# A planner that counts a delay between dependent instructions of one engine, in a fused attention and expert kernel

## The chip, the cores and the metric

The kernel runs on one core of a Trainium2 chip. A core has five engines that each work through their own queue of instructions in order: TensorE (PE, matmuls; its weight loads are listed apart as PEld), VectorE (DVE), ScalarE (ACT), GpSimd (POOL) and SyncE (SP, which here only starts transfers). They wait for one another through semaphores. The metric is the device time of one execution in microseconds (us).

## The reference

Three stages follow one another. All values are float32.

```python
# attention with decay: B=4, H=8, S=768, D=48
f = 1.0 / (1.0 + np.exp(-f_logit))
for t in range(S):
    state = f[:, :, t, :, None] * state + einsum('bhd,bhe->bhde', k[:, :, t], v[:, :, t])
    y[:, :, t] = einsum('bhd,bhde->bhe', q[:, :, t], state)
# feed-forward: x is 3072 x 384 (tokens x 8 heads of 48), w_in 384 x 2048, w_out 2048 x 384
h = x @ w_in
x = (maximum(h, 0) + alpha * minimum(h, 0)) @ w_out
# experts: 8 of them, each takes 384 tokens, w1 384 x 1024, w2 1024 x 384
logits = x @ w_gate
for idx in argsort(-logits.flatten()):        # best pairs first
    tok, e = idx // 8, idx % 8
    if tok is unassigned and counts[e] < 384: assign tok to e
out[tokens of e] = maximum(x[tokens of e] @ w1[e], 0) @ w2[e]
```

## The kernel before, in words

**How it is built.** The program is first recorded: every call (`nc.vector.tensor_tensor`, `nc.tensor.matmul`, ...) only makes an object `Op` with its dependences, its engine or two possible engines, a price in ns (`cost`) and a priority (`prio`, small is urgent). `Plan.schedule` then goes through all of them as a list scheduler: again and again it takes, over all engines, the instruction that can start first by its own model; of those that can start at the same time the one with the smaller priority. The order that comes out is the order of each engine's queue. No time of the model enters the program, only this order, the buffers, and which of two engines takes an instruction. An instruction is ready when its producers have ended plus `lag`: 110 to 200 ns where the producer is on another engine (`LAGS`), nothing where it is on the same one. All instructions are recorded through one lambda, so that the trace puts them all to line 206 (210 after the change); L1651 are warming matmuls on a tile of ones (`fill`), which the planner puts into gaps that it expects on PE, and L226 the rectifier.

**Precision.** Matmuls run in fp32r; a float32 operand is split into a high part and a low part (`split`: ScalarE copies the high part, then an engine subtracts it), and three products replace one. The subtraction may go to DVE or to POOL (`low`, `Plan.either`): the planner takes the one that it expects to end it first (`better`), where POOL costs 200 + 2.08 ns an element and DVE 66 + 1/0.96.

**Stages, with the times of the profile.** To about 140 us: attention in 24 chunks of 128 tokens (scans and products on DVE, small matmuls on PE), and beside it the preparation of the feed-forward weights in groups 0 to 7 (`prepare_in`, `prepare_out`): the raw weights are narrowed by two bit instructions each on DVE (`narrow`; SCALAR_TENSOR_TENSOR on `early`, `raw`), then split. `win0`, `wo0`, `win1`, `wo1` ... are the tiles `weights0`, `weights1`, `weights2`, `weights3` ...; `raw2` and `raw3` feed group 1. PE does the first blocks of the feed-forward as their weights come. From 140 to 530 us: blocks 0 to 6 of the feed-forward (384 tokens each): 9 matmuls give a piece of the hidden layer (`bank<-weights,rounded`), ScalarE and DVE rectify it (tile `common`), it is split into `rounded`, and 9 matmuls project it (`bank<-rounded,weights`). Beside it the expert weights are split and written to `wd` in DRAM.

From 530 us: the last block, whose logits come before its rows, and the routing. The assignment is found expert by expert in a chain: `bounds` finds the range of the logits (tile `mm`, two small matmuls with `ident`), then four counts follow, each a compare of all 3072 best logits with 64 thresholds on DVE (`cut`, 128x1536) and 12 matmuls that add them up (`bank<-late`), two matmuls with `pairs` and `ones`, and small DVE instructions; `take` writes the number of the expert, at which SP starts the load of its weights; `lists` makes the list of its tokens (DVE compares, 24 matmuls `bank<-late 128x6`, then `idx`). All these tiles lie in the arena `late`. POOL gathers the tokens from `x2d` in DRAM by `idx`; PE transposes them (`bank<-ident,common`). Experts 0 to 7 follow from 618 us; the chain runs two experts ahead of its use and the lists one ahead, in gaps between the expert's matmuls. The chain of expert 0 has nothing ahead of it but the rows of the last block.

**Priorities.** Attention 0 to 60 by block, weight preparation 15.5, expert p's matmuls 105 + 10p, its chain instructions (for p+2) 99 + 10p, its lists (for p+1) 98.5 + 10p, and what makes its hidden layer (`urgent`) 98 + 10p. Chain 0 has 81, the last block 80, its rows 84, and its hidden layer 70.

Of the kernel before, what the change touches and what calls it, by code (L numbers as in the profile page):

```python
# [71 lines left out]
LOADS = 2  # L72


WINDOW, BUSY = 10240 / 3, 3060.0

LAGS = {"tensor": 200.0, "vector": 165.0, "scalar": 150.0, "gpsimd": 110.0, "sync": 120.0}
# [62 lines left out]
class Plan:  # L140
# [181 lines left out]
    def schedule(self):  # L322
        self.layout()
        ops = self.ops
        for op in ops:
            op.left = len(op.deps | op.soft)
            for d in op.deps | op.soft:
                d.next.append(op)
        for op in ops:
            for a in op.arenas():  # L330
                a.left += 1
        free = dict.fromkeys(self.ENGINES, 600.0)
        free["tensor"] = 800.0
        avail = {e: [] for e in self.ENGINES}
        mm, hw, dma = [0.0, 0.0], 600.0, [0.0, 0.0]

        def offer(op):
            since = max([g.since for g in op.uses if g.slot] + [d.start for d in op.soft], default=0.0)
            op.ready = {e: max([d.end + lag(d, e) + (op.load if d in op.held else 0.0) for d in op.deps], default=since) for e in op.engines}
            for e in op.engines:  # L340
                avail[e].append(op)

        def first(op, e):
            t, taken = max(op.ready[e], free[e]), []
            for a in op.arenas():
                if any(o.left for o in a.over):
                    return None
                t = max([t] + [o.turn for o in a.over])
            for g in op.first:
                p = self.place(g, taken)  # L350
                if p is None:
                    return None
                t = max(t, p[0])
                taken.append(p[1])
            return t

        for op in ops:
            if not op.left:
                offer(op)
        for _ in ops:  # L360
            best = None
            for e in self.ENGINES:
                for op in avail[e]:
                    if best is not None and max(op.ready[e], free[e]) > best[0]:
                        continue
                    t = first(op, e)
                    if t is None or len(op.engines) > 1 and not self.better(op, e, t, free):
                        continue
                    key = (t, op.prio, op.idx)
                    if best is None or key < best[:3]:  # L370
                        best = key + (e, op)
            assert best, "no instruction can start"
            t, _, _, e, op = best
            for x in op.engines:
                avail[x].remove(op)
            for g in op.first:
                g.since, g.slot = self.place(g, ())
                g.slot.busy = True
                g.tag.given += 1
            price = op.cost[e]  # L380
            if e == "tensor":
                self.fill(free[e], t)
                slow = self.slow(t)
                if op.load:
                    mm[1] = max(mm) + op.load * slow
                    t = max(t, mm[1])
                price *= slow
                mm[0] = t
                self.count(t, t + price, op.columns)
            op.engine, op.start = e, t  # L390
            for a in op.arenas():
                a.left, a.turn = a.left - 1, max(a.turn, t + 1.0)
            free[e] = op.end = t + price
            if op.bytes:
                at = op.end
                if e == "sync":
                    hw = at = max(hw, at) + 450.0
                lane = e == "sync"
                dma[lane] = max(dma[lane], at + 650.0) + op.bytes / (300.0 if lane else 200.0)
                op.end = dma[lane] + 1000.0 + op.extra  # L400
            for g in op.uses:
                g.uses -= 1
                g.end = max(g.end, op.end)
                if not g.uses:
                    g.slot.busy, g.slot.free = False, g.end + 100.0
            for n in op.next:
                n.left -= 1
                if not n.left:
                    offer(n)
        return max(op.end for op in ops)  # L410
# [94 lines left out]
def lag(d, e):  # L505

    if d.bytes:
        return 0.0
    if d.engine == e:
        return 0.0  # L510
    return LAGS[d.engine] + (40.0 if e == "gpsimd" else 0.0)


# [1312 lines left out]
```

## Time and profile before

| | us |
|---|---|
| median of 3 runs | 872.51 (870.24 to 876.36) |
| the profiled execution, its own time | 872.57 |
| its span in the profile | 870.6 |
| PE busy | 829.7 |
| DVE busy | 580.2 |
| ScalarE busy | 350.9 |
| GpSimd busy | 118.6 |
| mean granted clock of PE | 0.979 of full |

Busy times add the instructions of an engine; matmuls overlap their neighbours, so a start-to-start distance says more than a duration where they stand in a row. In the rows of a timeline, the first number is the start in us from the beginning of the span, the second the duration (of the whole group where several instructions are put together as xN), then the engine, the line, the operation, output<-inputs by the names of their arenas, and in brackets how long the engine was idle before it and what ended that.

### The profile page before, as it was taken

The numbers are of one execution on the slowest core, as the hardware profiler recorded it, in microseconds if no ns is written. First come the engines' busy times: TensorE is split into PE (matmuls) and PEld (weight loads), VectorE is DVE, ScalarE is ACT, GpSimd is POOL, SyncE is SP. The second block draws the span as 40 slices with busy tenths as digits, with TensorE's granted clock in tenths as the row PEclk, the third lists the DMA queues.
The fourth block names the chain that finished last, engine by engine and source line by source line (L and its number), as shares of the span: only waits on it lengthen the run. The fifth ranks groups of instructions, "written<-read, shape, count | busy, mean of one in ns | idle before, by whom it ended". The sixth has DMA issues, their size and how long they took to land. (4 is left out here: it accounts for less than half of the span.)

```text
span 870.6 us, 16049 instructions
## 1 busy us (share of the span) xinstructions
PE 829.7 (95%) x6125; PEld 764.4 (88%) x6125; DVE 580.2 (67%) x1302; ACT 350.9 (40%) x742; POOL 118.6 (14%) x111
## 2 busy tenths in 40 slices
PE   6999899999999999999999999998799999999995
PEld 4677788999999999999999998986688998999995
DVE  6998996956966966966976644655677568553220
ACT  3456775455455455455554433510112222212220
POOL 3100321200300200200300100000203203202211
PEclk7999998999999999999999999999899999999998
DMA  8996112888798698688778710007467865777400
GB/s 173 277 278 146 28 28 76 203 294 279 197 298 274 143 303 285 177 297 274 231 266 271 244 64 28 1 10 308 151 261 301 313 245 180 274 275 251 165 28 31
DMA packets 92790, 172.60 MB, mean 198 GB/s; under 512 B 31672, under 2 KB 61376, under 8 KB 92704
## 3 DMA queue, kind: packets, MB, share of 16 engines
q1 hardware_dynamic: 89056, 161.45, 58.3%
q0 software_dynamic: 3072, 9.44, 3.1%
q8 instruction: 50, 0.82, 0.4%
q10 hardware_dynamic: 576, 0.60, 0.2%
q14 instruction: 36, 0.29, 0.1%
HBM read 111.69 MB, written 59.77 MB: 197 GB/s over the span
## 5 line engine op out<-in xcount | busy, mean ns | idle before, releaser
L206 PE MATMUL bank<-rounded,weights 128*128 128x384 f32 (+1 forms) x1740 | 356.7, 346 | 2.8 <-POOL weights L206 1.6
L206 PE MATMUL bank<-weights,rounded 128*128 128x392 f32 (+1 forms) x1620 | 326.7, 346 | 3.5 <-DVE weights L206 1.9
L206 PEld LDWEIGHTS bank<-rounded,weights 128*128 128x128 f32 (+1 forms) x1740 | 306.0, 189 | 10.6 <-issue 3.7
L206 PEld LDWEIGHTS bank<-weights,rounded 128*128 128x128 f32 x1620 | 289.0, 189 | 6.9 <-DVE weights L206 3.3
L206 ACT ACTIVATE rounded<-bank 128x384 fp32r<-128x384 f32 x110 | 53.8, 491 | 198.1 <-PE bank L206 188.3
L206 DVE TENSOR_TENSOR early<-early 128x384 fp32r<-128x384 f32 (+2 forms) x196 | 117.5, 621 | 18.2 <-ACT early L206 17.0
L206 PEld LDWEIGHTS bank<-early 128*64 128x64 f32 (+2 forms) x1696 | 99.0, 154 | 19.1 <-issue 9.2
L206 PE MATMUL bank<-early 128*64 128x128 f32 (+3 forms) x1696 | 111.7, 271 | 1.0 <-ACT early L206 0.5
L206 DVE SCALAR_TENSOR_TENSOR common<-common,rest,bank 128x384 f32<-128x384 f32 x128 | 77.9, 609 | 49.4 <-ACT common L226 48.9
L206 ACT ACTIVATE early<-early 128x384 fp32r<-128x384 f32 (+2 forms) x177 | 95.3, 546 | 37.1 <-DMA wd<-early 22.4
L206 POOL TENSOR_TENSOR rounded<-common,rounded 128x384 fp32r<-128x384 f32 x40 | 52.6, 1315 | 366.3 <-ACT rounded L206 308.5
L226 ACT ACTIVATE common<-bank 128x384 f32<-128x384 f32 x128 | 62.5, 488 | 83.1 <-PE bank L206 82.3
L206 ACT ACTIVATE rounded<-common 128x384 fp32r<-128x384 f32 x118 | 61.7, 523 | 65.7 <-DVE common L206 65.5
L206 DVE TENSOR_TENSOR_SCAN early<-early 128x516 f32<-128x516 f32 x48 | 64.2, 1337 | 2.3 <-ACT early L206 1.2
L206 DVE SCALAR_TENSOR_TENSOR rounded<-bank,rounded 128x384 fp32r<-128x384 f32 x62 | 34.3, 554 | 46.4 <-ACT rounded L206 44.0
L206 DVE TENSOR_TENSOR rounded<-common,rounded 128x384 fp32r<-128x384 f32 x78 | 44.3, 569 | 27.8 <-ACT rounded L206 22.5
L206 ACT ACTIVATE common<-bank 128x384 f32<-128x384 f32 x48 | 23.3, 491 | 72.8 <-PE bank L206 69.3
L206 POOL DMA_INDIRECT out_dram<-common,late x24 | 25.5, 1062 | 171.3 <-ACT common L206 137.4
L206 POOL DMA_INDIRECT common<-x2d,late x24 | 26.8, 1118 | 150.8 <-DMA weights<-wd 119.5
L206 DVE TENSOR_TENSOR late<-late,cols 128x1536 bf16<-128x1536 bf16 (+3 forms) x53 | 42.7, 821 | 1.0
L206 DVE TENSOR_TENSOR early<-bank,mask 128x512 f32<-128x512 f32 x48 | 30.9, 684 | 6.1 <-PE bank L206 6.0
L206 DVE TENSOR_TENSOR rounded<-bank,rounded 128x384 fp32r<-128x384 f32 x48 | 26.3, 553 | 12.9 <-ACT rounded L206 12.4
(110 smaller groups left out, 494.8 us busy)
## 6 DMA issues: line engine op xcount, KB each, us to landing
wd<-early SPq DMA_DIRECT2D x128, 384.0 KB, 3.3
weights<-wd SPq DMA_DIRECT2D x64, 768.0 KB, 5.4
early<-in_w_dram SPq DMA_DIRECT2D x64, 384.0 KB, 4.3
early<-in_fkq_dram SPq DMA_DIRECT2D x46, 288.0 KB, 4.9
raw<-in_w_in_dram SPq DMA_DIRECT2D x16, 384.0 KB, 6.8
raw<-in_w_out_dram SPq DMA_DIRECT2D x16, 384.0 KB, 8.0
early<-in_v_dram SPq DMA_DIRECT2D x24, 192.0 KB, 4.9
x2d<-common SPq DMA_DIRECT2D x21, 192.0 KB, 3.0
```

Source lines behind the costliest of these rows:

```text
L206: op = self.add(engines, lambda e, b: getattr(e, method)(*[b(x) for x in a], **{n: b(x) for n, x in k.items()}), outs, ins)
L226: return e.activation(b(out), b(x), AF.Relu, scale=-1.0)
```

## The change

Two things change, both in the planner. `lag` gives 125 ns between two dependent instructions on VectorE and 150 ns on ScalarE, where it gave nothing. And on VectorE the next instruction is chosen in another way: the planner looks at all instructions that could start within 170 ns (`PATIENCE`) of the one that can start first. If the most urgent of them has a priority of at least 80 (`URGENT`: the routing and the experts), is more urgent than the one that would start first, and would be held up by it by more than 60 ns, then the planner takes the first one that ends in time for it, or else the urgent one itself, and leaves the engine idle until then. No instruction of the computation is added or removed.

```diff
+SAME = {"vector": 125.0, "scalar": 150.0}
+PATIENCE = 170.0
+URGENT = 80.0
@@ in Plan.schedule
             for e in self.ENGINES:
+                wait, own, near = PATIENCE if e == "vector" else 0.0, None, []
                 for op in avail[e]:
-                    if best is not None and max(op.ready[e], free[e]) > best[0]:
+                    since = max(op.ready[e], free[e])
+                    if best is not None and since > best[0] or own is not None and since > own[0] + wait:
                         continue
...
-                    key = (t, op.prio, op.idx)
-                    if best is None or key < best[:3]:
-                        best = key + (e, op)
+                    key = (t, op.prio, op.idx, e, op)
+                    if wait:
+                        near.append(key)
+                    if own is None or key < own:
+                        own = key
+                if near:
+                    h = min((k for k in near if k[0] <= own[0] + wait), key=lambda k: k[1])
+                    if URGENT <= h[1] < own[1] and own[0] + own[4].cost[e] > h[0] + 60.0:
+                        fits = [k for k in near if k[0] + k[4].cost[e] <= h[0] + 60.0]
+                        own = min(fits, default=h)
+                if own is not None and (best is None or own < best):
+                    best = own
@@ in lag
     if d.engine == e:
-        return 0.0
+        return SAME.get(e, 0.0)
```

The order on DVE in the preparation, where group 1 of the weights is narrowed (`early<-early,raw2` and `early<-raw2,early` are the two bit instructions of one half of it; `weights2` is its split). Before:

```order
L206 SCALAR_TENSOR_TENSOR early_110<-early_110,raw2_166 128x384
L206 SCALAR_TENSOR_TENSOR early_110<-raw2_166,early_110 128x384
L206 SCALAR_TENSOR_TENSOR early_110<-early_110,raw2_166 128x384
L206 SCALAR_TENSOR_TENSOR early_110<-raw2_166,early_110 128x384
L206 TENSOR_TENSOR weights2_584<-early_110,weights2_584 128x384 x2
```

After the change:

```order
L210 SCALAR_TENSOR_TENSOR early_110<-early_110,raw2_166 128x384
L210 TENSOR_TENSOR early_110<-bank2_67,early_110 64x4x48
L210 TENSOR_TENSOR rounded_102<-common_106,rounded_102 128x384
L210 TENSOR_TENSOR early_110<-bank2_67,early_110 64x4x48
L210 TENSOR_TENSOR weights1_499<-bank0_65,weights1_499 128x2x8
L210 SCALAR_TENSOR_TENSOR early_110<-raw2_166,early_110 128x384
L210 SCALAR_TENSOR_TENSOR early_110<-early_110,raw2_166 128x384
L210 TENSOR_REDUCE turn_79<-early_110 128x1
L210 SCALAR_TENSOR_TENSOR early_110<-raw2_166,early_110 128x384
L210 TENSOR_TENSOR pairs_78<-pairs_78,early_110 128x128
L210 TENSOR_TENSOR weights2_591<-early_110,weights2_591 128x384 x2
```

Attention steps, a split of the hidden layer and constants now stand between the two instructions of each half.

The order on POOL in the same stage: its share of the splits (`weights` are weight splits, `rounded<-common` those of the hidden layer). Before:

```order
L206 TENSOR_TENSOR weights0_419<-early_110,weights0_419 128x384 x2
L206 TENSOR_TENSOR rounded_102<-common_106,rounded_102 128x384 x4
L206 TENSOR_TENSOR weights7_970<-early_110,weights7_970 128x384
L206 TENSOR_TENSOR rounded_102<-common_106,rounded_102 128x384
L206 TENSOR_TENSOR weights9_1081<-early_110,weights9_1081 128x384
L206 TENSOR_TENSOR rounded_102<-common_106,rounded_102 128x384 x2
L206 TENSOR_TENSOR weights10_1143<-early_110,weights10_1143 128x384
L206 TENSOR_TENSOR rounded_102<-common_106,rounded_102 128x384 x4
L206 TENSOR_TENSOR weights15_1412<-early_110,weights15_1412 128x384
```

After the change:

```order
L210 TENSOR_TENSOR weights0_403<-early_110,weights0_403 128x384 x2
L210 TENSOR_TENSOR weights1_499<-early_110,weights1_499 128x384 x2
L210 TENSOR_TENSOR rounded_102<-common_106,rounded_102 128x384 x2
L210 TENSOR_TENSOR weights3_664<-early_110,weights3_664 128x384 x2
L210 TENSOR_TENSOR weights5_794<-early_110,weights5_794 128x384
L210 TENSOR_TENSOR rounded_102<-common_106,rounded_102 128x384 x4
L210 TENSOR_TENSOR weights8_979<-early_110,weights8_979 128x384 x2
L210 TENSOR_TENSOR rounded_102<-common_106,rounded_102 128x384
L210 TENSOR_TENSOR weights9_1058<-early_110,weights9_1058 128x384 x2
L210 TENSOR_TENSOR rounded_102<-common_106,rounded_102 128x384
L210 TENSOR_TENSOR weights10_1122<-early_110,weights10_1122 128x384
```

POOL's weight splits go from 6 (to the group of `weights15`) to 12, more of them early.

The order on PE where `bounds` hands over to the first count, at about 536 us (`bank<-ident,common` are the two matmuls of `bounds`, the first `bank<-late 128x16` is the count). Before:

```order
L206 MATMUL bank_67<-ident,common 2x128
L206 MATMUL bank_71<-rounded,weights_419 128x384 x3
L206 MATMUL bank_72<-rounded,weights_419 128x384
L206 MATMUL bank_66<-ident,common 128x2
L206 MATMUL bank_72<-rounded,weights_419 128x384 x8
L1651 LDWEIGHTS ones
L1651 MATMUL bank_70<-ones 128x512
...
L206 LDWEIGHTS late
L206 MATMUL bank_65<-late 128x16
```

After the change:

```order
L210 MATMUL bank_66<-ident,common 2x128
L210 MATMUL bank_71<-rounded,weights_403 128x384
L210 MATMUL bank_72<-rounded,weights_403 128x384 x3
L210 MATMUL bank_65<-ident,common 128x2
L210 MATMUL bank_72<-rounded,weights_403 128x384 x6
...
L210 MATMUL bank_71<-rounded,weights_591 128x384 x5
...
L210 MATMUL bank_72<-rounded,weights_591 128x384 x3
L210 LDWEIGHTS late
L210 MATMUL bank_67<-late 128x16
```

Three warming matmuls are gone, and 26 matmuls of projections and logits stand between the first matmul of `bounds` and the count, where 12 stood.

The order on PE before the lists of expert 1 at about 621 us (`late,ones` and `late,tri` are the last two matmuls of its chain, `bank<-late 128x6` the first of its lists). Before:

```order
L206 MATMUL bank_66<-late,ones 128x24
L206 LDWEIGHTS tri
L206 MATMUL bank_66<-late,tri 128x24
L206 MATMUL bank_72<-rounded,weights_419 128x384 x6
L206 MATMUL bank_71<-rounded,weights_584 128x384 x9
L206 LDWEIGHTS late
L206 MATMUL bank_67<-late 128x6
```

After the change:

```order
L210 MATMUL bank_65<-late,ones 128x24
L210 LDWEIGHTS tri
L210 MATMUL bank_65<-late,tri 128x24
L210 MATMUL bank_71<-rounded,weights_591 128x384 x8
L210 MATMUL bank_69<-weights_979,rounded 128x384 x3
L210 MATMUL bank_70<-weights_979,rounded 128x384 x3
L210 MATMUL bank_68<-weights_979,rounded 128x384 x3
L210 MATMUL bank_72<-rounded,weights_591 128x384 x4
L210 LDWEIGHTS late
L210 MATMUL bank_66<-late 128x6
```

The lists stand behind 21 expert matmuls, where they stood behind 15.

## Rows read from the trace of the kernel before

**Rows 1.** The page's busy times: us, share of the span, instructions.
```profile
PE 829.7 (95%) x6125; PEld 764.4 (88%) x6125; DVE 580.2 (67%) x1302; ACT 350.9 (40%) x742; POOL 118.6 (14%) x111
```

**Rows 2.** Busy times by stage: stretch, us; each engine's busy us, instructions; PEclk, DMA, GB/s.
```profile
8.00:140.00 132.00, 116.78 (x893) 99.17 (x894) 117.83 (x220) 80.84 (x186) 19.68 (x18) 0.91 0.59 145
140.00:530.00 390.00, 389.94 (x2979) 373.76 (x2977) 278.67 (x499) 192.60 (x401) 39.85 (x29) 1.00 0.75 233
530.00:618.00 88.00, 80.42 (x538) 67.19 (x537) 49.01 (x147) 21.32 (x43) 3.02 (x3) 0.96 0.24 93
618.00:871.00 253.00, 236.75 (x1706) 222.16 (x1703) 129.01 (x418) 53.43 (x109) 49.29 (x45) 0.99 0.57 211
```

**Rows 3.** PE's waits from 8 to 140 us: releaser, us in total, times, longest.
```profile
PE bank L206 <- DVE early L206: 10.1, 5, 7.2
PE bank L206 <- DVE weights L206: 2.2, 3, 1.7
PE bank L206 <- POOL weights L206: 1.6, 1, 1.6
```

**Rows 4.** PE's waits from 530 to 600 us (three), then from 618 us on (three).
```profile
PE bank L206 <- DVE late L206: 1.1, 2, 0.9
PE bank L206 <- issue: 0.7, 1, 0.7
PE bank L206 <- DVE common L206: 0.5, 1, 0.5
...
PE bank L206 <- DVE late L206: 3.8, 8, 0.8
PE bank L206 <- DMA common<-x2d,late: 1.3, 4, 0.4
PE bank L206 <- DVE rounded L206: 1.1, 2, 0.6
```

**Rows 5.** PE's timeline at six places.
```profile
131.36 2.65 PE L206 MATMUL bank<-weights,rounded 128*128 128x392 f32 x7 [1.70 <-DVE weights L206]
...
540.48 0.40 PE L206 MATMUL bank<-late 128*128 128x16 bf16 x10 [0.74 <-issue]
...
612.74 0.90 PE L206 MATMUL bank<-ident,common 128*128 128x128 f32 x3 [4.57 <-DMA common<-x2d,late]
...
624.90 0.36 PE L206 MATMUL bank<-late 128*128 128x6 bf16 x8 [0.69 <-DVE late L206]
...
648.66 4.93 PE L206 MATMUL bank<-weights,rounded 128*128 128x384 f32 x27
...
655.78 0.39 PE L206 MATMUL bank<-late,pairs 128*128 128x8 f32 x2 [0.48 <-DVE late L206]
```

**Rows 6.** DVE's timeline in the preparation: start, duration, instruction.
```profile
46.34 0.56 DVE L206 SCALAR_TENSOR_TENSOR early<-raw,early 128x384 int32<-128x384 int32 x1
46.81 0.55 DVE L206 SCALAR_TENSOR_TENSOR early<-early,raw 128x384 int32<-128x384 int32 x1
47.40 0.56 DVE L206 SCALAR_TENSOR_TENSOR early<-raw,early 128x384 int32<-128x384 int32 x1
...
108.43 1.07 DVE L206 TENSOR_TENSOR weights<-early,weights 128x384 fp32r<-128x384 f32 x1
```

**Rows 7.** DVE's timeline in the routing chain: a small instruction, a compare, an unrelated one.
```profile
602.72 0.24 DVE L206 TENSOR_SCALAR late<-late,bank 128x24 bf16<-128x24 f32 x1 [0.31 <-PE bank L206]
603.00 0.96 DVE L206 TENSOR_TENSOR late<-late,cols 128x1536 bf16<-128x1536 bf16 x1
603.88 0.24 DVE L206 TENSOR_SCALAR late<-late,bank 128x24 f32<-128x24 f32 x1
```

**Rows 8.** POOL's timeline: a weight split beside DVE's of 108.43 us.
```profile
107.63 1.45 POOL L206 TENSOR_TENSOR weights<-early,weights 128x384 fp32r<-128x384 f32 x1 [1.70 <-ACT weights L206]
```

**Rows 9.** DMA issues from 590 to 613 us: count, KB each, us from issue to landing.
```profile
x2d<-common ACTq DMA_DIRECT2D x2, 192.0 KB, 8.2
```

**Rows 10.** The stretch from 130 to 138 us, columns as in rows 2.
```profile
130.00:138.00 8.00, 6.64 (x22) 6.64 (x23) 6.06 (x14) 4.77 (x10) 1.24 (x1) 0.57 0.00 0
```

## The prediction

> **What bounds the kernel now.** Read first the page's busy times [rows 1]: TensorE (PE) works 829.7 of 870.6 us. So PE's work cannot shrink through an order, and what can be won or lost is PE's idle time and its useless work (100 warming matmuls on `ones`). Next the busy times by stage [rows 2], to see where that lies. From 140 to 530 us PE is busy 389.94 of 390.00: nothing to win there whatever the others do. From 8 to 140 us it works 116.78 of 132, while VectorE (DVE) works 117.83: the stage in which weights are prepared beside the first attention chunks, and DVE sets its pace. From 530 to 618 PE misses 7.6 us, from 618 on 16.2, of which 6.2 are waits with a name (next paragraph); most of the rest lies behind its last matmul, where the last output is stored, which this change does not touch. There DVE is at 129.01 of 253: it is late in single places, not full.
>
> Then the waits of PE by stage. In 8 to 140 [rows 3]: 10.1 us for DVE's attention instructions, of which one of 7.2 is the start (DVE must first make chunk 0's operands), 2.2 for weights split on DVE, 1.6 for one split on POOL. In 530 to 600: 2.3 us in three rows; in 618 to the end: 6.2 us, 3.8 of it for DVE's routing chain [rows 4]. The hole of 4.57 us before 612.74 us is the gather of expert 0's tokens [rows 5].
>
> **The change, part by part.** The planner now waits 125 ns before it lets a DVE instruction start on the result of another DVE instruction (150 on ScalarE), so it puts independent work between the two. Is the delay real? In the prep, an instruction that reads what the one before it wrote starts 0.59 us after it (47.40), one that doesn't 0.47 (46.81) [rows 6]; in the chain, the first kind starts 0.04 us after the other's end, the second kind 0.08 us before it [rows 7]. So 0.12 us a pair.
>
> The Trainium skill ("VectorE: DVE Perf Modes", The DRAIN you can't avoid) says that the next DVE instruction waits for the pipe to empty and that leaving semaphores out between chained instructions gains nothing: by it the pairs of the prep would save 0 and not 3.8 us. The two rows just read disagree with it here, since the unrelated instruction does start before the end of the one ahead; its case is rival B.
>
> *Prep, 8 to 140 us.* In the order as planned, 34 DVE instructions there read the result of the one right before; 2 do after the change (the order on DVE in the section on the change shows four in a row drawn apart). Saved on DVE: 32 x 0.12 = 3.8 us. (In all stages 298 before and 133 after, but it counts only where PE waits for DVE.) The delay also moves splits to another engine: eleven go from DVE to POOL and six come back (weights on POOL: 6 splits before, 12 after, as the order on POOL shows). Each of the net five frees DVE of 0.47 us, but POOL took 1.45 us for the one at 107.63, and the DVE split beside it took 1.07 us, where an instruction of that size takes 0.55 [rows 6, 8]: 0.52 lost for 0.47 won. I put the net of this on DVE at nothing.
>
> PE gains what DVE gains only where it waits for DVE: past the start, 10.1 - 7.2 + 2.2 = 5.1 us of waits [rows 3]. Bounds -5.1 and 0. DVE is nearly full here, and the last weights are what PE waits for near the end of the stage (1.70 us at 131.36 [rows 5]); but part of what is saved lies between waits. I take half of 3.8: **-1.9**. Against it stands POOL: it now makes both low halves of `wo0`, `wo1`, `win4` and `wo4` and one of `wo2`, in order, with its share of the hidden layer between them. The one wait of this kind cost PE 1.6 us [rows 3]. Five tiles moved: bounds 0 and 5 x 1.6 = 8.0; PE has other work ordered before most of them, so one more such wait: **+1.6**.
>
> *530 to 600 us.* PE waits in turn for `mm` (0.5), for DVE's `late` tiles (1.1 in two) [rows 4] and for the first compare (0.74 at 540.48, put down to issue [rows 5], behind three warming matmuls). The new order puts projections of 0.18 us each (4.93 us for 27 at 648.66 [rows 5]) where the warming stood, 14 more ahead of the first compare by the order on PE, and makes DVE do the hidden layer's two instructions that feed PE first. To win: the 2.3 and up to 0.8 of warming, 3.1. Bounds -3.1 and 0; nearly all of it is covered by moved matmuls: **-2.6**.
>
> *The hole at 608.* The gather needs the last rows stored; the store took 8.2 us to land [rows 9], issued while expert 0's weights were on their way. Those weights start when chain 0 knows its expert. Its deciding matmul moves about seven matmuls (7 x 0.18 = 1.3 us) later in PE's stream, and the DVE instruction that writes the expert's number moves ahead of four others, of about 0.24 us each by [rows 7], 1 us earlier. Even: **0**. If the number came later and the store queued behind the weights, each us would cost one; bounds -1 and +1.
>
> *618 to the end.* For most experts the chain's matmuls move behind some 4 to 9 more expert matmuls (21 instead of 15 stand before the lists of expert 1, in the second order on PE), the urgent hidden-layer subtraction moves ahead of the chain's long compares on DVE (the `PATIENCE` rule: DVE may stay idle up to 170 ns for it, free on an engine busy half of the time), and the transposes behind a gather move some ten matmuls back. To win: 6.2 [rows 4], with the 0.69 at 624.9 before the lists of expert 1 and the 0.48 at 655.78 before a count [rows 5] among them; the longest, 0.8, has no expert matmul moved ahead of it. The price is a later chain; it is needed two experts, some 60 us, ahead, so that is hidden, and would cost its lateness if it were not. Bounds -6.2 and 0. Of the eight waits for `late`, three at the first count of a chain, like the 0.48, keep their neighbours (1.4); with the 0.8 and half a us of the gathers that is 2.7 left standing: **-3.5**.
>
> *ScalarE.* 18 of its instructions read what the one before wrote, 12 after the change; at DVE's 0.12 a pair that is 0.7 us on an engine that is busy 53.43 of 253 us from 618 on [rows 2]: 0, bounds -0.7 and 0.
>
> *Sum:* -1.9 + 1.6 - 2.6 - 3.5 = -6.4. The profiled execution took 872.57 us by its own time (span 870.6 and about 2 around it), equal to the median of 872.51. So **866.2 us**.
>
> **Rivals.**
> A, the sum: 862 to 869.5, centre 866.2.
> B, nothing arrives: the freed waits come back at the next dependent step, since PE's order is fixed and its work is 95% of the span. For it: PE is full for 390 us, and a chain that PE reaches later ends later. Against it: the waits named have independent matmuls in front of them now. Time 872.6 (870 to 875). This is also where the Trainium skill's rule on the drain ("VectorE: DVE Perf Modes", The DRAIN you can't avoid) ends: if every start waits for an empty pipe, the 32 pairs bring nothing.
> C, **slower: POOL becomes what PE waits for in the prep**. Place: the `wo` splits. Price: 5 x 1.6 = 8.0 on PE, and 5 x 0.5 = 2.5 that DVE loses to POOL's reads, +10.5; with none of the gains behind 530 us 883.1, with all of them (-6.1) 877.0. It decides from the point where POOL's second split of a tile ends after PE's last matmul ordered before it; a split took 1.45 us beside DVE's at 107.63 [rows 8], against 1.0 by the planner's price (200 + 2.08 x 384 ns).
> D, everything arrives: -5.1 - 3.1 - 6.2 = -14.4, 858.2, and with it some of the slow clock. The granted clock was 0.57 of full in 130 to 138 us, mostly the 1.2 GHz level, around PE's wait of 1.70 us [rows 5, 10]; if without that wait the stretch ran at 2.4 GHz, it would give up to 8 x 0.43 = 3.4 us more: 855.
>
> **How the numbers follow.** A 0.46, B 0.20, C 0.16, D 0.18. About 1% (8.7 us) is what a measurement here can tell from no change: faster than 863.8 is D and a third of A (0.16), 0.34; slower than 881.2 is about half of C, 0.08; the same is 0.58. The range leaves out D's lower part and C's upper half: 857 to 878.
>
> **What would show it.** Right: in 8 to 140 us DVE's busy time falls or its last weights split ends some 2 us earlier than 138; no idle of PE at 536 to 541 us; no wait of PE for the lists of expert 1 (0.69 at 624.9 us before); PE's waits behind 618 us under 3 us in sum. Wrong: waits of PE for POOL's weights of several us in 40 to 110 us (C); the waits for DVE's `late` tiles unchanged in sum but at other instructions (B); a low clock in a new stretch; expert 0's weights issued later relative to the last store, with a hole longer than 4.6 us.

## The result, and the profile after

The changed kernel takes 859.0 us (median of 4 runs, 858.42 to 861.39) against 871.92 for the kernel before (4 runs beside it and ahead of it): ratio 0.984, interval 0.9814 to 0.9865. On a second chip it was 858.85 against 873.32, ratio 0.983 (0.9802 to 0.9858). So it is 13 to 14.5 us faster, where 6.4 were forecast: right in direction, twice as large.

The profiled execution took 861.39 us (span 859.5). The busy times of its page, beside [rows 1]:

```profile
PE 825.2 (96%) x6123; PEld 760.2 (88%) x6123; DVE 563.2 (66%) x1301; ACT 349.8 (41%) x742; POOL 121.5 (14%) x112
```

VectorE has 17.0 us less to do for the same instructions but one, a subtraction that went to POOL. By stage, beside [rows 2] (the same windows, in which work now comes some 5 to 10 us earlier):

```profile
8.00:140.00 132.00, 117.88 (x920) 98.41 (x920) 116.54 (x216) 81.62 (x188) 31.89 (x24) 0.96 0.61 156
140.00:530.00 390.00, 389.76 (x2980) 374.69 (x2980) 274.45 (x510) 192.79 (x403) 29.99 (x21) 1.00 0.75 230
530.00:618.00 88.00, 82.48 (x561) 69.77 (x559) 51.85 (x168) 20.58 (x41) 5.56 (x5) 0.96 0.27 103
```

In the first stage PE does 920 matmuls where it did 893, at a mean granted clock of 0.96 where it was 0.91. PE's waits from 8 to 140 us, beside [rows 3] (us in total, times, longest):

```profile
PE bank L210 <- DVE early L210: 8.5, 6, 5.1
PE bank L210 <- ACT early L210: 1.8, 3, 0.8
PE bank L210 <- POOL weights L210: 1.1, 2, 0.7
PE bank L210 <- DVE rounded L210: 0.6, 1, 0.6
PE bank L210 <- DVE weights L210: 0.6, 2, 0.4
```

From 525 to 598 us (one row) and from 609 to 860 us (three), beside [rows 4]:

```profile
PE bank L210 <- DVE common L210: 0.3, 1, 0.3
...
PE bank L210 <- DMA common<-x2d,late: 2.0, 2, 1.6
PE bank L210 <- DVE late L210: 1.3, 5, 0.3
PE bank L210 <- issue: 0.6, 1, 0.6
```

And PE's timeline at the first count, the hole of the gather, the lists of expert 1 and a gather, beside [rows 5]:

```profile
536.27 0.40 PE L210 MATMUL bank<-late 128*128 128x16 bf16 x10
...
603.95 0.90 PE L210 MATMUL bank<-ident,common 128*128 128x128 f32 x3 [4.95 <-DMA common<-x2d,late]
...
617.47 0.36 PE L210 MATMUL bank<-late 128*128 128x6 bf16 x8
...
630.95 0.90 PE L210 MATMUL bank<-ident,common 128*128 128x128 f32 x3 [1.60 <-DMA common<-x2d,late]
```

The waits of 0.74 at the first count and 0.69 at the lists are gone; the hole is 0.4 us longer than before.

**Where the time went.** No matmul is added or removed, so the start of one and the same matmul can be set against its start in the kernel before. Five of them: the first transposes of the preparation (14.13 us before), a matmul of the second feed-forward block (164.98, when the weights are made), the first of `bounds` (536.02), the first transposes behind the gather (612.74) and the last matmul (861.20). The table gives the shift against the profiled execution before, in us, for this kernel and for those of the experiments (each run's own profiled execution). One profile says little about 2 us: behind 612 us kernels of one order differ by up to 3 us, e7 and e10 for instance, and e2, e4 and e7, which have the order of before up to 165 us, reach that matmul at -1.02, 1.11 and -1.89. So kernels are compared by the medians on one chip, further on.

| kernel | 14.13 | 164.98 | 536.02 | 612.74 | 861.20 |
|---|---|---|---|---|---|
| changed | -1.25 | -5.33 | -5.35 | -8.80 | -11.18 |
| changed, second chip | -0.80 | -6.18 | -6.23 | -9.67 | -13.12 |
| e1 delay in the preparation only | -1.22 | -6.59 | -6.66 | -6.44 | -7.15 |
| e2 delay and rule behind it only | 0.06 | -1.02 | -0.56 | -3.88 | -11.22 |
| e5 VectorE's delay alone | -1.27 | -1.80 | -2.24 | -5.67 | -12.96 |
| e7 before, warmed in the preparation | 0.05 | -1.89 | -1.89 | -1.66 | -4.07 |
| e10 before, splits moved | -0.14 | -2.80 | -2.86 | -2.39 | -1.84 |
| e11 changed, splits back | -1.75 | -4.58 | -3.61 | -6.86 | -10.35 |
| e13 before, all waits warmed | -0.22 | -4.73 | -4.73 | -4.16 | -7.96 |
| e14 changed, all waits warmed | -1.72 | -9.81 | -9.87 | -13.27 | -23.28 |

Read along the first row: 1.25 us at the start, 4.1 in the rest of the preparation, nothing in 370 us of feed-forward, 3.4 in the last block and the first chain, 2.4 in the experts. The forecast had -0.3 for the first two of these together, then 0, -2.6 and -3.5. In the two profiles of the changed kernel the whole miss lies ahead of 165 us. Where the clock is held up in both kernels (e14 against e13), the same subtraction gives -5.1 up to 165 us, 0, -4.0 and -6.2: there more than half of the miss lies ahead of 165 us, and the rest behind 536.

**What is new in that stage.** VectorE's end of the weight preparation, by the last `gate` columns it writes, in the kernel before:

```profile
144.94 0.17 DVE L206 TENSOR_TENSOR weights<-bank,weights 128x16 fp32r<-128x16 f32 x1 [1.95 <-ACT weights L206]
```

and in the changed one:

```profile
140.33 0.17 DVE L210 TENSOR_TENSOR weights<-bank,weights 128x16 fp32r<-128x16 f32 x1 [2.10 <-ACT weights L210]
```

It comes 4.6 us earlier. Up to there VectorE was busy 126.6 us before and is busy 122.4 now (overlaps counted once, summed over the trace), and idle 18.5 and 18.1. In this pair of executions it gave on in full what it saved; the runs without half clock, further on, show that this is not the rule.

PE's clock in three stretches that were at the lower of its two levels, 1.2 GHz of 2.4, before (columns as in [rows 2]), in the kernel before:

```profile
93.00:96.00 3.00, 3.00 (x10) 3.00 (x11) 2.93 (x5) 2.00 (x5) 0.55 (x1) 0.50 0.00 0
110.00:113.00 3.00, 3.00 (x11) 3.00 (x10) 2.92 (x7) 2.82 (x8) 0.00 (x0) 0.51 0.01 3
131.00:137.00 6.00, 5.64 (x17) 5.64 (x18) 4.61 (x10) 3.88 (x9) 0.97 (x1) 0.50 0.00 0
```

and in the changed one:

```profile
93.00:96.00 3.00, 3.00 (x19) 3.00 (x18) 3.00 (x4) 2.25 (x6) 0.71 (x1) 1.00 0.00 0
110.00:113.00 3.00, 2.88 (x21) 2.63 (x19) 2.88 (x6) 2.92 (x8) 1.68 (x1) 1.00 0.83 197
131.00:137.00 6.00, 6.00 (x39) 5.75 (x37) 4.99 (x11) 4.53 (x12) 1.01 (x1) 1.00 0.61 123
```

Here 10, 11 and 17 matmuls stood in the time of 19, 21 and 39. The changed kernel has such stretches elsewhere (0.50 from 34 to 40 us, from 604 to 610 and, behind the wait of 1.60 at 630.95, from 631 to 634). So there are two candidates for the 5 us: the new order with VectorE's shorter work, and PE's clock. The first runs separate the stages, the others these two.

### The profile page after: what moved, and what is told of

Read it like the earlier page. It is cut to its first block, busy times and chain, and to the rows that moved or that the text cites. A ratio compares the mean times of both kernels' runs of the same rounds, so it can differ in the third digit from the quotient of the medians.

```text
span 859.5 us, 16037 instructions
## 1 busy us (share of the span) xinstructions
PE 825.2 (96%) x6123; PEld 760.2 (88%) x6123; DVE 563.2 (66%) x1301; ACT 349.8 (41%) x742; POOL 121.5 (14%) x112
## 5 line engine op out<-in xcount | busy, mean ns | idle before, releaser
L210 DVE TENSOR_TENSOR early<-early 128x384 fp32r<-128x384 f32 (+2 forms) x196 | 119.3, 625 | 11.4 <-ACT early L210 10.9
L210 POOL TENSOR_TENSOR rounded<-common,rounded 128x384 fp32r<-128x384 f32 x35 | 48.1, 1376 | 419.0 <-ACT rounded L210 380.2
L210 DVE TENSOR_TENSOR rounded<-common,rounded 128x384 fp32r<-128x384 f32 x83 | 47.6, 574 | 30.4 <-ACT rounded L210 22.0
L210 DVE TENSOR_TENSOR rounded<-bank,rounded 128x384 fp32r<-128x384 f32 x48 | 26.3, 552 | 12.7 <-ACT rounded L210 12.5
```

The source lines that it names most:

```text
L210: op = self.add(engines, lambda e, b: getattr(e, method)(*[b(x) for x in a], **{n: b(x) for n, x in k.items()}), outs, ins)
```

## The experiments

**The stages apart.** One theory: the gains of the stages add up, as the shifts of one matmul do. The rival: one only fills what the other leaves. e1 has the delay behind instructions of priority under 60 alone, and no rule; e2 the delay behind those of 60 and more, with the rule.

```diff
 e1:
-        return SAME.get(e, 0.0)
+        return SAME.get(e, 0.0) if d.prio < 60.0 else 0.0
-PATIENCE = 170.0
+PATIENCE = 0.0
 e2:
-        return SAME.get(e, 0.0)
+        return SAME.get(e, 0.0) if d.prio >= 60.0 else 0.0
```

> The delay only behind instructions of priority under 60 (attention, weight preparation, feed-forward); routing and experts are planned without it and without the rule on urgent instructions. If the stages add up as the two traces put them (5.4 us won by the end of the preparation, 5.7 behind 530 us), this gains 5.4 of the 13: about 866.5, from 864 to 868. If the gain of the preparation only came because later stages took it up (a chain that starts earlier), it gains under 2: above 870.

> The reverse: the delay only behind instructions of priority 60 and more, with the rule on urgent ones; the preparation keeps the order of before. If the stages add up: about 866, from 864.5 to 867.5, with PE's clock in the preparation as before (four stretches at half). If my prediction's sizes behind 530 us were right (2.6 + 3.5 = 6.1): 865.8, the same; what tells it from a rival is the sum of this run's gain and that of the preparation alone: 11 to 13 if they add up, well under 11 if one hides the other.

Measured on one chip: e1 866.51 against 870.45, ratio 0.9952 (0.9929 to 0.9975); e2 861.68, ratio 0.9894 (0.9833 to 0.9956). The gains are 3.9 and 8.8, in sum 12.7: as far as the intervals tell (2.2 to 6.2 and 3.8 to 14.5 us), they add up to the whole change. e1 came out as expected; e2 did not, it gained more than the 864.5 to 867.5 expected and more than the 6.1 us forecast for its part. In e2 PE does not wait for the routing chain any more behind 618 us; the only row of waits left there is

```profile
PE bank L210 <- DMA common<-x2d,late: 2.7, 5, 1.5
```

**PE's clock by itself.** In e7 the order of the kernel before is kept, and 23 warming matmuls are put at four of its waits in the preparation; `WARM` counts them by the instruction that waited, and the diff is the same in all warmed kernels.

```diff
+WARM = {355: 3, 967: 4, 954: 8, 1056: 8}
@@ in Plan.schedule
                 self.fill(free[e], t)
+                for _ in range(WARM.get(op.idx, 0)):
+                    s = next((s for s in self.bank_slots if not s.busy and s.free <= t), None)
+                    if s is not None:
+                        f = Op(len(self.ops) + len(self.fills), ("tensor",), [lambda e, b, k=s.at // 2048: self.filler(e, k)], 0.0)
+                        f.engine, f.start, f.end = "tensor", t - 0.001, t
+                        self.fills.append(f)
```

> The kernel before with 23 more warming matmuls, put ahead of four matmuls in the preparation at which PE waited in its trace (3 at 89.8 us, 4 at 104.7, 8 at 109.1, 8 at 131.4): work on PE where it was idle, nothing else moved. If the half-clock stretches that followed these waits (3.4, 3.4 and 6.9 us) cost the time: two or three of them go and the kernel gains 3 to 6 us, 866 to 869. If DVE sets the pace of the stage and PE's clock is hidden behind it: no change, 872, or up to 2 us slower where the warming runs past the wait.

Measured: 867.92 against 870.45, ratio 0.9978 (0.9953 to 1.0003): 2.5 us, at the lower edge of what the clock theory wanted and just inside what noise allows. The three stretches did go:

```profile
93.00:96.00 3.00, 3.00 (x17) 2.49 (x17) 2.93 (x6) 3.00 (x10) 1.99 (x1) 1.00 0.00 0
110.00:113.00 3.00, 3.00 (x18) 2.58 (x17) 2.93 (x6) 2.48 (x6) 0.49 (x1) 1.00 0.00 0
131.00:137.00 6.00, 6.00 (x34) 5.42 (x32) 5.12 (x11) 4.61 (x11) 0.64 (x1) 1.00 0.00 0
```

With 12 us of the preparation back at full clock, up to 6 us could have come; 1.9 came by 165 us. But e7 was already 1.5 us behind the kernel before at the matmul of 85.11 us, ahead of its first warming matmul, so that 3.4 came from there on. Not all that a stretch gave back was kept: 1.0 us won at the matmul of 95.21 us is gone at that of 105.13. The warming did not run past three of its four waits: there the waiting matmul starts 0.05 us after the end of the instruction that it waited for, as in the kernel before (the trace names none for the fourth). So the clock is worth something, but less than its rows say: a part goes back into waits for the other engines.

**Which part of the planning did it.** e3 has no rule (PATIENCE 0), e4 the rule without any delay (SAME empty), e5 the delay on VectorE alone, and e6 is a control: the kernel before, with VectorE dearer by the same total in the plan, but everywhere alike.

```diff
 e3:
-PATIENCE = 170.0
+PATIENCE = 0.0
 e4:
-SAME = {"vector": 125.0, "scalar": 150.0}
+SAME = {}
 e5:
-SAME = {"vector": 125.0, "scalar": 150.0}
+SAME = {"vector": 125.0}
 e6, in cost() of the kernel before:
-        return 66.0 + n / (1.92 if fast else 0.96) + 60.0 * scalars
+        return 95.0 + n / (1.92 if fast else 0.96) + 60.0 * scalars
```

> All delays, but the rule on urgent instructions off (PATIENCE 0). If the delay is the whole cause: 859, within 1 us. If the rule brings the urgent hidden-layer instructions ahead of compares for PE, as the prediction had it: PE's waits from 618 us on go up by some 2 us, 861.

> The rule on urgent instructions without any delay. If the delay is what moves the order, 0, within 1.5 us of the kernel before at the same granted clock; if the rule alone brings part of the gain behind 530 us, 2 us or more under it there.

> The delay on VectorE alone, none on ScalarE. My prediction put ScalarE's at nothing: then 857 to 861, as the changed kernel. If ScalarE's order in the preparation matters (the planner puts 7 weight splits on GpSimd instead of 12 and 124 warming matmuls instead of 98, and by its own clock ends 6.6 us later): 3 us or more slower than the changed kernel.

> A control on the kernel before: no delay between dependent instructions, but 29 ns more on the planner's price of every VectorE instruction (1302 x 29 ns = 37.8 us, as much as 298 pairs x 125 ns), so that the planner is as pessimistic about VectorE but not told where. If the gain comes from knowing which instructions have to wait: little of it, 867 to 873. If any slower VectorE in the plan would do (more splits on GpSimd, the chain's matmuls later): most of it, 858 to 863.

| kernel | us | before, same chip | ratio (interval) |
|---|---|---|---|
| e3 no rule | 854.36 | 870.45 | 0.9813 (0.9763 to 0.9864) |
| e4 rule without delay | 872.64 | 873.32 | 0.9985 (0.9962 to 1.0008) |
| e5 VectorE's delay alone | 861.80 | 873.36 | 0.9869 (0.9819 to 0.9918) |
| e6 uniform price | 870.64 | 873.32 | 0.9964 (0.9947 to 0.998) |
| changed, again | 858.85 | 873.32 | 0.983 (0.9802 to 0.9858) |

> The changed kernel itself once more, on one chip with the three below and with the kernel before, to compare them at the same granted clock. Expected: 13 us under the kernel before, ratio 0.984 to 0.987. If what the runs of one kernel differ by is the time at half clock, its time falls by 0.8 to 0.9 us for each 0.001 of the mean granted clock, as it does for the kernel before (875.9 us of span at 0.975, 865.6 at 0.986).

The rule alone does nothing, and the kernel without it is not slower. e3 even came out 4.6 us under the 859 expected; below, on one chip and with all waits warmed, nothing of that is left. Over 64 runs of the kernel before the time falls by 0.53 us for each 0.001 of the clock, not by the 0.8 to 0.9 expected with the second run of the changed kernel. The uniform price brings 2.7 of the 14.5 us: it is not enough that the plan is pessimistic about VectorE, it must know where. Without ScalarE's delay the gain is 11.6 on its chip, some 2.4 to 3.3 us less than the changed kernel's ratios would give there; the intervals overlap, so a loss is not shown. If there is one, its profile puts it in the preparation (-1.80 at 165 us where the changed kernel has -5.33; at the last matmul it is as early as the changed one), where the plan puts 7 weight splits on POOL instead of 12 and has 124 warming matmuls instead of 98.

**The splits on POOL.** e10 is the kernel before with the 19 splits of the preparation that changed their engine put where the changed kernel has them; e11 is the reverse. `TAKE` names them by number: 12 go to POOL and 7 to VectorE, not 11 and 8 as the expectation has it (the first three of 19 are shown).

```diff
 e10 (e11 with the two engines exchanged, on the changed kernel):
+TAKE = {777: 'vector', 247: 'gpsimd', 249: 'gpsimd',
...
     def better(self, op, e, t, free):
+        if op.idx in TAKE:
+            return e == TAKE[op.idx]
```

> The kernel before, without delay and rule, but with the 19 splits of the preparation that changed their engine put where the changed kernel has them (11 from VectorE to GpSimd, 8 back). The rest is planned as before. If GpSimd's share is what made the preparation shorter: most of the 4 us of the preparation alone, 866 to 868, with fewer stretches at half clock. If the delay between dependent instructions did it: no gain, and what my prediction feared of GpSimd (waits of PE for its weights, up to 8 us) shows here if anywhere: 870 to 877.

> The reverse: the changed kernel with the same 19 splits on the engines of before. If the splits' move is the cause in the preparation, it loses 3 to 5 us against the changed kernel: 861 to 863. If the delay is: within 1.5 us of it, 857 to 860.

Measured on one chip (before 873.36): e10 870.14, ratio 0.9954 (0.993 to 0.9978); e11 861.74, ratio 0.9844 (0.9801 to 0.9887). The moved splits alone win 3.2 us (1.9 to 6.1 by the interval), with as much time at half clock as before; without them the delay still wins 11.6. Neither expectation holds as it stood: both parts bring something. And PE does not wait for POOL in e10. All its waits from 15 to 140 us:

```profile
PE bank L207 <- DVE early L207: 5.4, 4, 2.8
PE bank L207 <- DVE weights L207: 3.5, 3, 1.6
PE bank L207 <- issue: 1.5, 1, 1.5
PE bank L207 <- ACT early L207: 1.1, 1, 1.1
PE bank L207 <- ACT weights L207: 0.9, 2, 0.8
```

No row names POOL. VectorE's end of the preparation comes at 140.7 us in e10 instead of 145.1, with 121.3 us of work up to there instead of 126.6 (125.0 in e2 and e7, which have the order of before there).

**Both kernels without half clock.** What is left: how much of the whole is the clock. e13 warms all long waits of the kernel before, e14 those of the changed kernel, e12 those of the changed kernel without the rule (e9 only the hole of the gather, without the rule).

```diff
 e9:  +WARM = {5274: 22}                                                    (and PATIENCE = 0.0)
 e12: +WARM = {72: 22, 181: 6, 171: 3, 5274: 22}                            (and PATIENCE = 0.0)
 e13: +WARM = {72: 31, 181: 6, 355: 3, 967: 4, 954: 8, 1056: 8, 5274: 20}   (the kernel before)
 e14: +WARM = {72: 22, 181: 6, 171: 3, 5274: 22}
```

> The changed kernel with PATIENCE 0 and with 22 warming matmuls ahead of the transposes behind the first gather, where PE stood idle for 4.9 us (22 x 0.216 = 4.75 us) and then ran at half clock for 6.8 us. If that stretch is due to the idle time: it goes, -2.5 us from the clock, and with the rule off as fast as or faster than without the rule: 849 to 853. If PE behind the gather waits for ScalarE and DVE anyway: no change from the kernel without the rule, 854.

> The changed kernel with the rule off, 22 warming matmuls in the hole of the first gather and 31 more at three waits near the start (22 ahead of the first transposes, where PE stood 5.1 us, 6 and 3 at the waits of 1.46 and 0.76 at 32.3 and 33.7 us). If the stretches at half clock there (6.8 us at 11 us, 3.4 at 35 us) come from the idle time ahead of them and cost PE time: 2 to 4 us under the same kernel without these 31, 851 to 853. If DVE sets the pace near the start: no change, 855, or slower where the 22 run at half clock past the wait.

> The kernel before with 80 more warming matmuls at all its long waits: 31 ahead of the first transposes (7.2 us idle), 6 at 31.2 us, the 23 of the run that warmed the preparation, 20 in the hole of the first gather. If its stretches at half clock cost what their rows say (9.6 us in the preparation, 0.5 and 2.7 around and behind the gather) and all of them go: about 860, with a granted clock of 0.995 or more. If part of the clock is hidden behind VectorE: 863 to 868.

> The changed kernel, with its rule on urgent instructions, and 53 more warming matmuls at its long waits (22 ahead of the first transposes, 6, 3, and 22 in the hole of the gather). With no stretch at half clock left in either kernel, the difference to the kernel before with its warming is what the order alone brings: 6 to 8 us if my rows behind 530 us are right (3.4 and 3 to 4 us there, none in the preparation but about 1 at the start), 3 or less if the clock made most of the gain. By itself: 852 to 855.

> The same as the run above with the rule on urgent instructions off, on one chip with it. My prediction called the rule free. If it is: the same within 0.6 us. If it costs the expert stage time (VectorE idles up to 170 ns ahead of an urgent instruction, and the chain's small matmuls come late): 1 to 2.5 us faster than with the rule.

| kernel | us | before, same chip | ratio (interval) | granted clock |
|---|---|---|---|---|
| e9 no rule, gather warmed | 855.41 | 873.32 | 0.9794 (0.9769 to 0.9819) | 0.991 |
| e12 no rule, all warmed | 853.10 | 873.36 | 0.9757 (0.9716 to 0.9799) | 0.997 |
| e13 before, all warmed | 864.90 | 871.48 | 0.9926 (0.9897 to 0.9955) | 0.997 |
| e14 changed, all warmed | 850.18 | 871.48 | 0.9772 (0.9738 to 0.9807) | 0.996 |
| e12 again | 851.03 | 871.48 | 0.9766 (0.9737 to 0.9795) | 0.989 |

(The clock is that of the profiled execution; e12's second one was one with two stretches at half, 856.94 us; its other six runs took 850.03 to 851.80.) In e9 the clock behind the hole of the gather stays up, where that of the changed kernel on the same chip fell. e9:

```profile
600.00:606.00 6.00, 5.46 (x31) 2.85 (x30) 1.85 (x6) 0.98 (x2) 2.84 (x3) 1.00 0.37 104
606.00:612.00 6.00, 6.00 (x48) 5.33 (x46) 4.66 (x21) 1.47 (x3) 0.00 (x0) 1.00 0.01 3
```

The changed kernel:

```profile
600.00:606.00 6.00, 2.93 (x13) 2.25 (x14) 0.86 (x5) 0.75 (x2) 2.85 (x3) 0.59 0.36 104
606.00:612.00 6.00, 6.00 (x41) 4.91 (x40) 3.91 (x15) 1.22 (x3) 0.00 (x0) 0.84 0.01 3
```

e9 came to 855.41 and not to the 849 to 853 expected: by the ratios (0.9794 and 0.9813 for e3) the warming of the gather alone is not shown to win anything.

With no stretch at half in either profile, the orders differ by 864.90 - 850.18 = 14.7 us, on one chip: as much as without any warming. That is twice the 6 to 8 us that I expected. e13 came out in the second of its two ranges (863 to 868, part of the clock hidden behind other engines), e14 under its range of 852 to 855. So the gain does not hang on the clock. Nor did the warming hold e13 up where it stands: at six of its seven warmed waits the waiting matmul starts as soon after the instruction that it waited for as in the kernel before (0.06 us or less, and behind the gather PE still waits 0.87 us); at the seventh, of 104.69 us, it starts some 0.5 us later.

The clock also rose on its own, from a mean of 0.981 in 64 runs of the kernel before to 0.986 in ten of the changed one. At 0.53 us for each 0.001 that would be some 3 us of the 13, and would leave 10 for the order. But warming brought e13 6.6 us for 0.016 and e14 some 7.3 for 0.010, so one slope does not hold for both orders, and the clock's share of the 13 cannot be read off it.

**Which engine sets the pace of the preparation.** VectorE's last `gate` columns once more, in e13:

```profile
140.22 0.17 DVE L207 TENSOR_TENSOR weights<-bank,weights 128x16 fp32r<-128x16 f32 x1 [1.94 <-ACT weights L207]
```

and in e14:

```profile
135.86 0.17 DVE L211 TENSOR_TENSOR weights<-bank,weights 128x16 fp32r<-128x16 f32 x1 [2.10 <-ACT weights L211]
```

The kernel before, e4, e2, e7 and e13 have one and the same order on VectorE up to there. It ended at 145.1, 146.2, 144.1, 143.2 and 140.4 us, with 126.6, 125.7, 125.0, 125.0 and 124.8 us of work, the earliest where PE's clock was never down. So VectorE waits for PE as PE waits for VectorE, and 1.6 of the 4.2 us of work that VectorE saved further up belong to that one execution of the kernel before. From e13 to e14 VectorE's work falls by 2.5 us and its end comes 4.4 us earlier; the rest is idle time (15.6 us, then 13.8). What made that shorter was not tried apart.

The rule on urgent instructions is free: 850.18 with it and 851.03 without, on one chip with all waits warmed.

e14 and e12 beat both kernels, by 20 to 21 us against the kernel before and, by its ratio of 0.984, by some 7 against the changed one.

## Why the prediction was wrong in size

**The price of a pair: right.** VectorE's busy time fell by 17.0 us with 165 pairs fewer (298 to 133), 0.10 us each. In the trace 801 of its instructions now start before the one ahead has ended, where 637 did, 164 more, and 12.3 of the 17.0 us is this overlap; the rest is instructions that took less time. In the preparation 33 more overlap, by 2.5 us in all; the 0.04 us that a dependent one stands still is idle time and not in this sum. So the 3.8 us for 32 pairs is borne out as a price, but the 4.2 us by which VectorE's work fell there is not a measure of it. The Trainium skill ("VectorE: DVE Perf Modes", The DRAIN you can't avoid) says that the next instruction does not start until the pipe is empty, by which the pairs would bring nothing, and adds that one that is not held starts earlier; the 801 early starts agree with the addition. Rival B, which took the first for every start, fell.

**The preparation: wrong, and this is the step that failed.** It was put at -1.9 for VectorE and +1.6 for POOL, -0.3 in sum; -5.3 came in the changed kernel's profile, -6.2 on the second chip, -3.9 by the medians with the delay in the preparation alone (e1), and -5.1 between e13 and e14, where no clock was down. Three terms were mis-sized.
- "I take half of 3.8": about all of it arrived behind the start, 4.1 us in the changed kernel's profile and 3.6 between e13 and e14, with what the moved splits won in it. The step bounded the gain by PE's 5.1 us of waits for VectorE past the start. They went only to 4.6 [rows 3 and the rows after], and yet VectorE ended 4.6 us earlier. The two engines wait for each other all through the stage, so that wait rows of one bound neither. Of the 4.4 us by which VectorE's end moves between e13 and e14, 2.5 are its shorter work; the cause of the rest stays open.
- "one more such wait: +1.6" for POOL: the waits for its weights went from 1.6 to 1.1 [rows 3], and the moved splits alone (e10) made the kernel 3.2 us faster. POOL's 12 weight splits take 1.38 us on average, nearly the 1.45 feared, but no long wait of PE followed, and VectorE's work up to the end of the preparation fell to 121.3 us in e10. Rival C fell.
- "past the start": the wait of 7.2 us was taken as fixed. It is 5.1 now, and 6.7 on the second chip, where the operands came later. With the delay counted, the planner puts the product for chunk 0 between the reciprocal and the scan that needs it, and the first transposes start 1.25 us earlier (0.80 there).

The clock was in the forecast only as 3.4 us of rival D, for one of four stretches. The stretches at 93, 110 and 131 us went, and others came. e4 has the three again and e2, with the same order, only one of 3.4 us, so they are not a matter of the order alone; all three together cost 3.4 us (e7). e13 and e14 show that the clock is not the main cause.

**530 us to the gather: right.** -2.6 forecast, -3.4 measured, -3.3 with the delay there alone (e2), -4.0 between e13 and e14. The waits of [rows 4] are down to 0.3.

**The hole: right.** 0 forecast; the idle time went from 4.57 to 4.95 us.

**The experts: the mechanism right, the size within the run's spread.** -3.5 forecast; -2.4 in the profile, with one stretch at half (631 to 634 us) that the kernel before did not have, -3.5 on the second chip, but -7.3 in e2 and -6.2 between e13 and e14 (-10.01 and -3.80 by the table). PE's waits behind the gather fell from 6.2 to 3.9 us, not under 3 as the forecast wanted; the 2.7 us of waits that it left standing can go too: of those for `late` none is left in e2 and e14. The rule costs nothing, as said, but brings nothing either.

**ScalarE: open.** Put at 0, bounds -0.7 and 0, from its pairs. Leaving its delay out (e5) costs 2.4 to 3.3 us against the changed kernel by the medians, which is not clear of noise. The forecast looked at the pairs alone and not at the splits and the warming that the planner then places otherwise.

**The rivals.** D, that everything arrives, -5.1 - 3.1 - 6.2, was the nearest, with 0.18. Its second term came as it stood (-3.4), and its third does in e14. That its first agrees (-5.3) is in part luck: it was to be PE's waits for VectorE, and these are still there. I gave it too little since I took half of each freed wait as lost to the next one, with no row that showed such a loss. Two of the signs of being wrong did appear, though small: a low clock in new stretches (34 to 40 and 631 to 634 us) and a hole longer than 4.6 us (4.95).

## What to carry to other kernels

Where two engines are both nearly full, the wait rows of one do not bound what a saving on the other brings: here 5.3 us came by 165 us while those waits fell by 0.5. Follow one and the same matmul through several runs instead. A planner's model gains from knowing where an engine has to stand still (here 0.12 us between dependent instructions), and not from a general surcharge of the same sum (2.7 of 14.5 us). Where waits of the matmul engine can't be removed, matmuls on ones that fill them keep its clock up, here for another 7 us.

## What the runs showed of the hardware that was not expected

Runs of one and the same kernel differ by up to 10 us on one chip, with the mean granted clock: the spans of the kernel before went from 875.9 us at 0.975 to 865.6 at 0.986. And three kernels that are planned alike up to 165 us (the changed one, e1 and e3) reached that matmul at -5.33, -6.59 and -9.52 us, with 10.2, 10.2 and 3.4 us at half clock up to there: the stretches at half clock fall at other places and in other numbers from one execution to the next, so that one profile says less of a stage's clock than it seems to.
